# A written-out step list drawn up anew, with 38 constant products at PE's start in place of 28

## The chip, the cores and the metric

The kernel runs on one core of a Trainium2 chip. Its time is the device time of one execution in microseconds (us). The engines are PE (TensorE, matrix products), ACT (ScalarE), DVE (VectorE), POOL (GpSimd) and SP (SyncE, which here only issues transfers). Each engine works through its own instructions strictly in the order in which they were written down, and waits on semaphores for the others.

## The reference

```python
x = A_x                                              # 2048 x 512, bf16
g = sigmoid((x * gate_w).sum(-1, keepdims=True))
# a: state space layer with 512 complex states
Lam_bar = exp(dt * Lam);  Bu = x @ B_bar.T
h[t] = Lam_bar * h[t-1] + Bu[t]                      # t = 0 .. 2047
a = 2.0 * (h @ Cmat.T).real + x * Dskip
# b: linear attention, 32 heads of 16, softmax features
q, k, v = split(x @ wqkv);  pq, pk = q @ w_phi, k @ w_phi    # per head
phi = concat(softmax(p), softmax(-p))                # for q and for k
kv = phi_k.T @ v;  z = phi_k.sum(seq)
b = (phi_q @ kv / (phi_q @ z + 1e-6)) @ wo
return g * a + (1 - g) * b
```

## The kernel before

The sequence is cut into 16 tiles of 128 rows. The rows are dealt out by their index modulo 8 (r = 0..7), so that the recurrence runs over chunks of 8 steps: within a chunk it is made of matrix products, and only the last step of each chunk goes through a scan on DVE.

The work is cut into small generator steps, and each token of the string `ORDER` (line 24) runs the next piece of one step. The order of the tokens is thus the order of every engine's instructions, of SP's transfers too; a scheduler changes nothing on PE, DVE, ACT and SP. A token can carry the PSUM banks (`@6`), and an engine: `:D` puts the evacuation of that piece on DVE in place of ACT, `:A` sends an output through ACT's queue in place of SP's. The loop that does it:

```python
for tok in ORDER.split():
    tok, _, eng = tok.partition(":")
    tok, _, banks = tok.partition("@")
    sel["eng"] = "dve" if eng == "D" else "act"
    sel["q"] = nc.scalar if eng == "A" else nc.sync
    sel["banks"] = [int(b) for b in banks]
    if tok == "F":
        for _ in range(int(eng)):
            MM(out=spin[:, 0:P], lhsT=fillw[:], rhs=fillw[:], start=True, stop=True)
        continue
    next(st[tok])
```

The steps that the prediction names, with their lines in the profile:

- `F:n` (L829): n products of a constant tile with itself, whose results nobody reads.
- `W0..W3` (L277, evacuated at L121 on ACT or L123 on DVE): transposes of the weights of k, in tiles `ptw`, into a part of `Xq`. `f0..f3` (L434): products of these with the block matrix `BD`, in tiles `pf`, evacuated by ACT into `Wk`. `f1` needs `W1` alone, and so on; a `k` needs all four. `w0..w3` are the same for q, from weights that the transfers `Q0..Q3` (L295) bring into `HM`; each `w` needs all four `Q`.
- `V`, `V2` (L313, L320): transposes of the small parameter vectors `vec_n`, `vec_m`, in tiles `pvt`.
- `l8..l15` (L232): transposed loads of x into `xT`, issued by SP. Tiles 0 to 7 are loaded ahead of the list.
- `k0..k15`, `q0..q15` (L478, 4 products of 512 columns): features of keys and queries. `v0..v15` (L492): the values.
- `grj` (L614, L619, L621): input products of the recurrence into `pgq`, from the transposed weights `BT` that the transfers `R0..R7` (L291) bring. `hrj` (L685): the states. `yn` (L734, L739): the output of the state space layer into `py`.
- `xn`, `nn`, `en`, `sn` (L519 to L567): the softmax features of a group of tiles of k; `X`, `N`, `E`, `S` those of q. In `S`, ACT takes a logarithm `lgq` and an exponential `rhoq` (L140), and after `rhoq` DVE scales `EEq` (L567); the result is transposed into `phT`, by SP's transfers (L579) or, for tiles 14 and 15, by PE (`pht`, L574).
- `an` (L594): the sums of the linear attention into `kvacc`.
- `on`: per tile two groups of products `pn` (L753), ACT's logarithm `ld` and exponential `rd` (L140), a cast `nu`, DVE's product `on` (L761), and its transpose `oT` by SP (L775) or PE (`po`, L770). `tn`: the last products `py<-Wo,oT` (L782), the scaling by the gate into `ot` (L786 on ACT, L788 on DVE), and the output transfer (L790).
- `C`, `J`, `c` (L299, L304, L603): the output weights of the state space layer, loaded, rearranged and scaled.

Of the kernel before, what the change touches and what calls it, by code (L numbers as in the profile page):

```python
# [23 lines left out]
ORDER = """
NI l8 l10 F:28 W1@0 W0@1 W0 B W2@2 W2 NR W1:D W3@3 f1@4 f1 W3:D V@5 V U f0@6 U P P P2 U P2 P2 P2 P2 f0 f2@0 P4 P4 P4
V2@1 V2 f2 l9 P3 i3 f3@3 f3 F:4 k1@2 k0@4 P P2 P3 l12 i1 i0 k0 gw i0 i3 U k1 i3 i3:D i3 i0 i1 i1 k2@5 k2 k3@6 k3 v0@03
k4@1 i0:D x0 i1:D l11 x0 i1 n0 F:4 x0 k4 n0 R0 i2 n0 i0 x0 n0 k5@4 i2 i2 x0 i2:D n0 x1 x1 k5 n1 i2 v3@25 v0 x1 k7@6 k7
k6@7 R1 L e0 n1 n1 x1 n1 l13 k6:D v4@14 x1 l14 v1@03 v1 k10@6 n1 x2 v4 n2 n2 n2 x2 e0 s0 x2 v3 v7@70 v7 l15 k8@3 v2@14
v6@25 s0 s0 k9@7 k12@0 x2 Q1 e1 s0 v2 v6 s0 k11@1 s0 e1 M k11 k8 D k10 k9 R3 k12 g40@4 g40 s0 s1 g00@2 g00 n2 a0@51 a0
v5@36 v5 s1 R5 x2 v8@70 R2 v8 C5 s1 s1 s1 s1 g60@4 n2 x3 s1 g60 g30@2 x3 n3 x3 n3 g10@3 C3 g20@6 e2 e2 e2 e2 x3 a1 a1  # L30
n3 Q2 k15@7 g10 g10 k15 x3 n3 g20 k14@0 k14 s2 n3 R4 s2 k13@4 g01@3 Q0 k13 n4 s2 g30 g01 x4 s2 x4 Q3 n4 x4 g50@7 g70@6
g30 g50 n4 x4 e3 e3 g41@0 g50 n4 R7 s2 g21@4 s2 g70 s2 C7 e3 g31@3 e3 s3 g62@2 C4 g70 g70 z0 g11@7 a2 z0 s3 g41 z0 a2
a2 s3 C6 g21 g62 C2 C1 g11 g11 C0 J0 w0@6 w1@0 J2 J2 a2 g22@4 J0 w2@2 x4 s3 J1 g31 w1 w0 w3@7 g22 g31 z0 z0 z0 s3 w2
s3 n4 z0 z0 w3 g61@0 g51@6 g51 g61 g02@4 g51 e4 g02 g71@3 g71 g71 g71 q3@2 s3 g12@7 g12 e4 q2@0 z0 g12 z1 q3 q1@6 q1
q0@4 q2 z1 z0 h50@3 z1 z1 g42@7 q0 z1 z1 v10@26 h50 xA z1 h10@0 e4 e4 z1 g42 nA s4 g32@4 v10 g32 a3 g52@3 g32 h60@7 c2
xA s4 c4 O g52 xA c4 R6 z1 z1 v9@26 s4 h10 g52 nA g72@4 g72 c4 h60 v9 a3 J3 g03@3 v11@26 c2 c2 s4 g72 g72 c0 c0 nA
g63@0 z2 z2 v12@74 a3 nA v11 a3 xA g03 z2 z2 z2 z2 xA nA s4 J3 g63 g23@2 c5 s4 v12 g23 h51@6 g13@3 g13 g13 z2 z2 c0 z2
z2 eA g43@0 g43 eA v14@74 v14 J1 h51 s4 g33@2 g33 h52@3 g33 h12@0 g53@6 eA g53 g53 h12 h11@7 h11 h52 eA sA g73@4 g73
g73 g73 v13@26 v13 q10@0 z3 c6 z3 c5 sA z3 z3 v15@73 z3 a4 a4 a4 v15 z3 q10 q5@4 a4 Y z3 h31@0 q5 sA h30@4 z3 q9@2 h31
q13@6 h31 q9 h33@0 h61@7 Y q13 h30 sA sA c5 h62@3 z3 z3 h30 h61 sA Y Y h22@5 q4@2 h62 q4 h33 q15@6 q11@7 h22 h20@4 h20  # L40
h32@2 h32 sA sA c1 q11 h13@1 h13 h32 q14@3 h40@5 h33 c3 h53@7 h42@4 sA h42 h53 c1 c1 sA h21@2 c3 h21 q6@0 q6 q15 c6
q7@1 h63@4 h63 q8@7 h03@0 c3 q7 c6 h40 sA c7 h41@6 h41 y6@2 c7 h03 h03 h43@4 h43 y2@1 h02@5 c7 sA h23@6 h23 h01@0
h00@4 END q8 G X1 y6 y6 q14 y2 N1 X1 h00 h00 N1 y2 h02 h02 X1 N1 G h01 o0@6 y0@7 o0 o0@3 h01 o2@4 o2 X1 o2@5 o2 o2 N1
y5@6 o0 y3@0 X1 N1 y5 X2 o0 o1@4 E1 o2 y0 o2 o0 E1 E1 E1 X2 y1@5 y1 y3 y3 o1 G N2 X2 N2 X2 o0 N2 X2 o3@3 o3 o3@4 S1 o3
o3 G S1 N2 S1 t2 o3 S1 o3 t2 t2:A q12@3 q12 N2 S1 S1 o1@4 o1 o1 o1 o1 S1 S1 E2 S1 y0 y4@1 y9@3 y8@4 y8 y8 X3 E2 E2 S1
S1 S1 N3 X3 E2 t3 X3 X3 X3 S2 N3 t0 t0 t0:A S2 t3 S2 y1 t1 t1 y5 y9 y9 o4@7 o4 o4@0 o4 y4 o4 o4 o4 o5@5 o5 o5@7 o5 o5
y13@0 S2 S2 o6@5 o6 o6@7 o6 o6 y13 N3 y7@5 y7 N3 y7 y13 o5 S2 S2 N3 E3 o5 o6 o6 S2 S2 E3 E3 o7@7 o7:D y4 t4 t4:D t5
o7@7 S2 S2 E3 S3 t5 S2 S3 S3 o7 o7 o7 t6 y11@1 y11 o7 t6 o8@6 o8 o8@7 o8 o8 S3 S3 o8 y12@2 o9@6 o9 o9@7 o8 y11 y12 y12
y10@6 o9 o9 o9 o11@7 o11 o9 S3 S3 y10 y10 o11@7 t7 o11 o11 t7 t8 S3 S3 o11 o11 S3 t8 S3@7 S3:D S3@5 S3 t9 t9 t1:A
o10@4 y15@7 o10:D o10@5 o10:D t8 o10 o10 o10 y15 o12@4 o12:D o12@3 t4 o14@5 o12 o12 o12 t5 o14 t11 o14@4 o14:D o14 o14  # L50
t11 y14@3 t9:A o13@5 o13 o12@4 o12:D y14 o13@1 o13 o13 o15@4 o15:D o15@5 o15 o15 t12 t3:A t10 o13 o13@1 o15 t6:A t11
o14@4 o13:D t7 t10 t10 y15 t12 t12 o15@5 o15 y14 o14:D t13 t14 t14 t14 t13 t13 t15 t15 t15:A
"""
# [811 lines left out]
```

## Time and profile before

| | us |
|---|---|
| median of 3 runs | 155.99 (155.83 to 156.77) |
| span of the profiled execution | 153.7 |
| PE, ACT, DVE, POOL busy | 145.5, 136.7, 131.0, 12.9 |
| TensorE clock granted, mean over the span | 0.995 |

The page gives the profiled execution its span, from the first to the last instruction of the core, and no time of its own. The runs lie 2.3 us above that span; what is counted there is outside the core's instructions. In a timeline, each row has a start, a length, an engine, a line, an operation, the tiles it writes and reads, and in brackets how long its engine stood idle before it and who ended that. PEld is the loading of PE's stationary operand, and names that end in q (SPq, ACTq) are the engines' transfer issues. Matmuls overlap, so a busy PE in a timeline need not be at its peak.

### The profile page before, as it was taken

What the parts mean: (1) busy time and instruction counts of PE and PEld (TensorE: products, weight loads), DVE (VectorE), ACT (ScalarE), POOL (GpSimd) and SP (SyncE); (2) the same over time, 40 slices, a digit from 0 to 9 for tenths busy, and PEclk for the clock granted to TensorE, in tenths of its full rate; (3) what the DMA queues carried; (4) which work ended last, traced back from release to release, by engine and by line L of the source; (5) the groups of instructions that cost most, each with busy time, mean ns of one, the idle gap of its engine ahead of it and who ended that gap; (6) DMA issues with size and microseconds to landing.
All of it is one profiled execution on the core that took longest, in us unless ns stands there. A gap on an engine that the chain in (4) does not pass through costs nothing.

```text
span 153.7 us, 3412 instructions
## 1 busy us (share of the span) xinstructions
PE 145.5 (95%) x1238; PEld 99.7 (65%) x1254; DVE 131.0 (85%) x302; ACT 136.7 (89%) x322; POOL 12.9 (8%) x43
## 2 busy tenths in 40 slices
PE   7799999999999999999999999999999899999990
...
DVE  3599999999999999999999999999999858445510
ACT  3599999999999999999999999999798897577672
...
GB/s 117 162 220 121 213 171 102 102 86 92 101 102 100 80 146 205 237 133 0 2 4 2 0 0 134 125 18 68 33 82 118 215 80 194 141 118 172 211 123 102
DMA packets 48737, 17.03 MB, mean 111 GB/s; under 512 B 42064, under 2 KB 48720, under 8 KB 48720
## 3 DMA queue, kind: packets, MB, share of 16 engines
...
q8 instruction: 10, 0.16, 0.5%
...
q14 instruction: 7, 0.06, 0.1%
...
## 4 chain that ended last, share of the span: by engine, by line
ACT 48%; PE 31%; DMA 8%; DVE 6%; issue 3%; POOL 2%; ACTq 0%; POOLq 0%
PE py L734 12%; ACT EEk L140 12%; ACT uv L121 9%; PE py L782 6%; ACT vx L121 5%; PE pq L478 5%; ACT Xq L121 5%; ACT phT L603 4%; PE ph L685 3%; ACT va L121 3%; DMA phT<-EEq 3%; DMA oT<-on 3%; PE pn L753 2%; DMA vec_n<-in_A_log_dt_dram 2%; ACT EEq L140 2%
## 5 line engine op out<-in xcount | busy, mean ns | idle before, releaser
L614 PE MATMUL pgq<-xT,BT 128*128 128x256 bf16 x256 | 31.5, 272 | 0.0
L614 PEld LDWEIGHTS <-BT 128*128 128x128 bf16 x256 | 24.7, 98 | 3.5
L140 ACT ACTIVATE EEk<-EEk 128x1024 bf16<-128x1024 bf16 x20 | 21.3, 1099 | 0.0
L478 PEld LDWEIGHTS <-xT 128*128 128x128 bf16 x128 | 12.2, 97 | 11.0 <-issue 0.2
L121 ACT CAST uv<-pgq 128x512 bf16<-128x512 f32 x28 | 16.7, 638 | 0.0
L492 PE MATMUL pv<-Wv,xT 128*128 128x256 bf16 (+1 forms) x128 | 16.5, 273 | 0.1
L478 PE MATMUL pq<-Wq,xT 128*128 128x512 bf16 x60 | 15.2, 379 | 0.2
L782 PE MATMUL py<-Wo,oT 128*128 128x512 bf16 x59 | 14.7, 379 | 0.6 <-DMA oT<-on 0.3
L478 PE MATMUL pk<-Wk,xT 128*128 128x512 bf16 x60 | 14.9, 379 | 0.2
L492 PEld LDWEIGHTS <-xT 128*128 128x128 bf16 x128 | 12.5, 98 | 3.1 <-issue 0.2
L786 ACT ACTIVATE ot<-py,G 128x512 bf16<-128x512 f32 x15 | 9.8, 684 | 2.9 <-PE py L782 2.4
L140 ACT ACTIVATE EEq<-EEq 128x1024 bf16<-128x1024 bf16 x12 | 11.8, 1084 | 0.3 <-DVE EEq L535 0.3
L603 ACT ACTIVATE phT<-X,dgB 128x512 bf16<-128x512 bf16 x16 | 11.1, 751 | 0.0
L140 ACT ACTIVATE ld<-pn 128x16 f32<-128x16 f32 x32 | 6.4, 204 | 5.2 <-PE pn L753 5.0
L121 ACT CAST vx<-pv 128x256 bf16<-128x256 f32 x32 | 10.7, 435 | 0.0
L121 ACT CAST nu<-pn 128x256 bf16<-128x256 f32 x26 | 10.0, 400 | 0.0
L556 DVE TENSOR_TENSOR EEk<-EEk,rck 128x4096 bf16<-128x4096 bf16 (+1 forms) x5 | 9.3, 1860 | 0.1
L121 ACT CAST Xq<-pq 128x512 bf16<-128x512 f32 x16 | 9.0, 604 | 0.4 <-PE pn L753 0.4
L782 PEld LDWEIGHTS <-oT 128*128 128x128 bf16 x64 | 5.7, 98 | 5.7 <-DMA oT<-on 0.5
L753 PEld LDWEIGHTS <-phT 128*128 128x128 bf16 x128 | 6.4, 97 | 4.6 <-DMA phT<-EEq 1.3
L761 DVE TENSOR_TENSOR on<-nu,rd 128x512 bf16<-128x512 bf16 x16 | 6.6, 422 | 2.6 <-ACT rd L140 2.1
L519 DVE TENSOR_TENSOR smk<-smk 128x512 bf16<-128x512 bf16 (+4 forms) x18 | 8.1, 449 | 0.1
...
## 6 DMA issues: line engine op xcount, KB each, us to landing
...
```

Source lines behind the costliest of these rows:

```text
L121: nc.scalar.copy(out=out_ap, in_=in_ap)
L140: ins = nc.scalar.activation(**kw)
L478: MM(out=pt[:], lhsT=xT[:, kt, ti * P:(ti + 1) * P], rhs=W[:, kt, :], start=(kt == 0), stop=(kt == KT - 1))
L492: MM(out=pv[c][:], lhsT=xT[:, kt, ti * P:(ti + 1) * P], rhs=Wvg[:, kt, c * hd:(c + 1) * hd + c], start=(kt == 0), stop=(kt == KT - 1))
L519: VT(out=dst, in0=cur[:, :, :, 0:n, :], in1=cur[:, :, :, n:2 * n, :], op=op)
L556: VT(out=E5, in0=E5, in1=rc.to_broadcast([P, L, 2 * NB, Dh, 4]), op=ALU.mult)
L603: nc.scalar.mul(out=t_, in_=x_, mul=c_)
L614: MM(out=pg[:, h, :], lhsT=BT[:, kt, 2 * j + h, :], rhs=xT[:, kt, r * NC:(r + 1) * NC], start=(h == 0 and kt == 0), stop=(r % 2 == 0 and k ...
L734: MM(out=py[:], lhsT=hs(r, t, slice(a * P, (a + 1) * P)), rhs=C2B[t], start=(t == 0), stop=False)
L753: MM(out=pn[:, 4 * m:4 * m + 4, :].rearrange("p h e -> p (h e)"), lhsT=ph[:, 4 * hf + m, :], rhs=KVm[:, 4 * hf + m, :], start=(m == 0), st ...
L782: MM(out=py[:], lhsT=oT[:, g, :], rhs=Wo[:, g, :], start=False, stop=(g == HG - 1))
L786: nc.scalar.mul(out=ot[:], in_=py[:], mul=G[:, ti:ti + 1])
```

## The change

Only the string `ORDER` differs. It still has 865 tokens, and every step has the same pieces. What differs is their order, the PSUM banks, the engine of 20 pieces, the queue of 4 outputs, and the first count of constant products:

```diff
-NI l8 l10 F:28 W1@0 W0@1 W0 B W2@2 W2 NR W1:D W3@3 f1@4 f1 W3:D V@5 V U f0@6 U P P P2 U P2 P2 P2 P2 f0 f2@0 P4 P4 P4
...
-o14@4 o13:D t7 t10 t10 y15 t12 t12 o15@5 o15 y14 o14:D t13 t14 t14 t14 t13 t13 t15 t15 t15:A
+NI B F:38 W0@5 W0 W1@2 W1:D W2@6 W2:D W3@2 W3:D f1@1 f1 l10 V@0 V U f3@6 P f0@4 f3 P f0 l8 f2@3 f2 NR l9 l12 l11 U P2
...
+o13 t10:D t12 o15@1 t13 t12:D t12 o15:D o14 t14 t10:A t14:D t13 t13:A t3:A t15 t15:D t4 t15:A t14
```

By its tokens, the evacuation of `W2` goes from ACT to DVE. In the last stretch the scaling of `t4` comes to ACT, that of `t8` to `t12`, `t14` and `t15` goes to DVE, and some casts and copies of `o7`, `o10` and `o12` to `o15` change sides. Of the seven outputs in ACT's queue, those of `t9` and `t6` change places with those of `t10` and `t13`.

**ACT at the program's start.** `ptw` are the transposed weights of k (`W`), `pf` the folded ones (`f`). Before:

```order
L132 ACT_TABLE_LOAD
L121 COPY Xq<-ptw 128x4x128 x2
L121 CAST Wk_78<-pf 128x512
L140 ACTIVATE ssm_par<-vec 128x4
L121 CAST Wk_78<-pf 128x512 x3
L140 ACTIVATE ssm_par<-ssm_par 128x4
```

Now:

```order
L132 ACT_TABLE_LOAD
L121 COPY Xq<-ptw 128x4x128
L121 CAST Wk_78<-pf 128x512
L140 ACTIVATE ssm_par<-vec 128x4
L121 CAST Wk_78<-pf 128x512 x3
L140 ACTIVATE ssm_par<-ssm_par 128x4
```

One of ACT's two evacuations of `W` is gone (DVE has three now, not two), and the rest of this stretch stands as it stood. On PE, the 16 products of `W` and the 16 of `f` follow the 38 constant products; `V` stands behind four products of `f` as before, and `V2` behind all sixteen, not behind twelve.

**SP's queue, from the eighth of the x tiles on.** `xT<-in_A_x_dram` are the `l` transfers, `BT<-Bn` the `R`, `HM<-in_B_wqkv_dram` the `Q`. Before:

```order
L287 DMA Bn<-in_A_B_re_dram 64x8x512
L232 DMA_TRANSPOSE xT<-in_A_x_dram 128x4x128 x3
L291 DMA_TRANSPOSE BT<-Bn 128x4x128 x2
L232 DMA_TRANSPOSE xT<-in_A_x_dram 128x4x128 x3
L295 DMA_TRANSPOSE HM<-in_B_wqkv_dram 128x512
L291 DMA_TRANSPOSE BT<-Bn 128x4x128 x3
L299 DMA_TRANSPOSE HM<-in_A_C_im_dram 128x512 x2
L295 DMA_TRANSPOSE HM<-in_B_wqkv_dram 128x512
```

Now:

```order
L287 DMA Bn<-in_A_B_re_dram 64x8x512
L232 DMA_TRANSPOSE xT<-in_A_x_dram 128x4x128 x3
L291 DMA_TRANSPOSE BT<-Bn 128x4x128 x2
L232 DMA_TRANSPOSE xT<-in_A_x_dram 128x4x128
L295 DMA_TRANSPOSE HM<-in_B_wqkv_dram 128x512 x2
L291 DMA_TRANSPOSE BT<-Bn 128x4x128 x2
L232 DMA_TRANSPOSE xT<-in_A_x_dram 128x4x128 x2
L295 DMA_TRANSPOSE HM<-in_B_wqkv_dram 128x512
L299 DMA_TRANSPOSE HM<-in_A_C_re_dram 128x512
L295 DMA_TRANSPOSE HM<-in_B_wqkv_dram 128x512
```

The last two tiles of x (first `l15`, then `l14`) stand behind four other transfers that they stood ahead of, or that stood further back; the fourth `Q` is the tenth transfer from `l13` on, where it was the thirteenth.

**ACT near the end, in the last group of query features.** `lgq` and `rhoq` are the logarithm and exponential of that group, `ld`, `nu`, `rd` those of a tile of `o` (tile numbers differ between the programs). Before:

```order
L140 ACTIVATE lgq_2237<-smq1_2188 128x256
L140 ACTIVATE ld_2247<-pn_2249 128x16
L121 CAST nu_2246<-pn_2249 128x256
L140 ACTIVATE ld_2247<-pn_2256 128x16
L121 CAST nu_2246<-pn_2256 128x256
L140 ACTIVATE rd_2248<-ld_2247,nge_85 128x128
L140 ACTIVATE ld_2286<-pn_2288 128x16
L121 CAST nu_2285<-pn_2288 128x256
L140 ACTIVATE rhoq_2299<-dlq_2297 128x128
```

Now:

```order
L140 ACTIVATE ld_2254<-pn_2256 128x16
L121 CAST nu_2253<-pn_2256 128x256
L140 ACTIVATE lgq_2275<-smq1_2196 128x256
L140 ACTIVATE ld_2254<-pn_2267 128x16
L121 CAST nu_2253<-pn_2267 128x256
L140 ACTIVATE rd_2255<-ld_2254,nge_85 128x128
L140 ACTIVATE rhoq_2295<-dlq_2293 128x128
L140 ACTIVATE ld_2300<-pn_2302 128x16
```

`rhoq` now stands ahead of the following tile's first `ld`, not behind it and its cast.

More of the change, by code (lines that the diff above doesn't have):

```diff
@@ L24 @@
 ORDER = """
-NI l8 l10 F:28 W1@0 W0@1 W0 B W2@2 W2 NR W1:D W3@3 f1@4 f1 W3:D V@5 V U f0@6 U P P P2 U P2 P2 P2 P2 f0 f2@0 P4 P4 P4
[L26 to L49, printed above, removed]
@@ L50 @@
-o10@4 y15@7 o10:D o10@5 o10:D t8 o10 o10 o10 y15 o12@4 o12:D o12@3 t4 o14@5 o12 o12 o12 t5 o14 t11 o14@4 o14:D o14 o14
-t11 y14@3 t9:A o13@5 o13 o12@4 o12:D y14 o13@1 o13 o13 o15@4 o15:D o15@5 o15 o15 t12 t3:A t10 o13 o13@1 o15 t6:A t11
-o14@4 o13:D t7 t10 t10 y15 t12 t12 o15@5 o15 y14 o14:D t13 t14 t14 t14 t13 t13 t15 t15 t15:A
+NI B F:38 W0@5 W0 W1@2 W1:D W2@6 W2:D W3@2 W3:D f1@1 f1 l10 V@0 V U f3@6 P f0@4 f3 P f0 l8 f2@3 f2 NR l9 l12 l11 U P2
+P2 P2 R0 R1 U l13 P2 P2 Q1 Q0 P4 P P3 P4 V2@0 F:4 V2 P4 U i3 i1 R2 i0 gw k0@6 k1@4 P2 k0 R3 l15 i0 k1 i3 i3 i0 k2@2
@@ new lines @@
+l14 i1 k3@5 i3:D i1 v0@10 n0 i3 x0 n0 k3 k4@6 v0 x0 i2 F:4 k5@1 P3 k6@3 Q2 k2 x0 C0 k4 n0 v1@06 i0:D i0 x0 n0 x0 k5 i2
+x1 i1:D i2 i1 i2:D i2 Q3 n0 x1 L C3 n1 k6:D n1 x1 k7@4 k7 n1 v3@71 x1 n1 x1 n1 R4 n2 R5 x2 C4 v4@25 v1 k8@3 e0 v7@40
+e0 n2 v4 C5 x2 v7 k10@6 k8 M s0 s0 v3 v2@25 x2 C7 s0 n2 s0 s0 D C6 v2 k9@0 k9 v6@43 s0 s0 k12@5 e1 e1 k12 k11@7 g40@2
+g40 v6 g00@0 s1 a0@51 s1 k11 n2 s1 R6 a0 g00 x2 s1 k10 v5@42 x2 g60@7 n2 x3 s1 v5 g20@6 n3 s1 s1 g60 v8@20 x3 n3 e2 e2
+g01@3 g10@4 a1 v8 a1 x3 e2 e2 g10 n3 k15@2 x3 C2 n3 k14@7 g20 k13@0 x3 g30@6 g10 k14 g30 k15 s2 s2 g01 n3 g50@2 s2 k13
@@ new lines @@
+n4 g30 w0@7 s2 e3 g50 x4 C1 g50 n4 J0 x4 J1 n4 J2 x4 J3 s2 s2 e3 e3 e3 g21@4 s2 g11@6 g31@3 n4 s3 x4 g70@0 s3 g70 g70
+g70 g41@2 a2 g11 g41 a2 a2 z0 z0 a2 g62@0 s3 w1@2 g21 z0 s3 g22@4 g11 g31 w1 s3 g62 w0 g31 x4 s3 z0 z0 z0 g61@6 w2@2
+w2 g61 g51@0 g51 g51 w3@3 w3 n4 e4 g71@7 g71 z0 z0 g71 g22 q1@6 g71 q0@0 s3 q0 q2@2 z0 q2 q1 g02@3 z1 g02 z1 q3@0 z0
+z1 q3 J2 J0 g12@7 e4 J3 g12 z1 z1 z1 g12 nA xA v10@64 z1 z1 g42@3 nA h50@2 h50 e4 e4 h10@0 h10 v10 s4 z1 z1 xA g32@7
+g32 g42 s4 g52@2 J1 v9@60 c4 g32 g52 h60@3 c2 h60 s4 v9 nA g52 g72@4 h51@6 h51 c4 c5 xA g72 v11@02 g72 h11@3 c4 a3 s4
@@ new lines @@
+a3 a3 v11 h11 xA g72 z2 z2 a3 nA c2 R7 g03@0 v12@74 xA nA g63@2 s4 c0 c0 g03 g63 v12 eA g23@3 g23 g13@0 g13 z2 h61@6
+z2 z2 s4 c2 g43@4 g13 z2 g43 eA g33@7 g33 g33 v14@34 v14 g53@0 c0 z2 z2 eA h61 g53 z2 g53 z2 s4 eA h52@7 h52 g73@6 g73
+h12@3 g73 q10@4 g73 sA q10 h31@4 h62@0 h62 v13@27 c6 z3 sA v13 h12 z3 h32@3 q9@6 sA q13@0 a4 z3 q9 h31 h31 v15@72 a4
+h32 c5 z3 v15 z3 z3 sA h22@6 h32 z3 z3 a4 q5@4 q13 q5 h22 h41@7 a4 Y c3 q4@2 q4 z3 z3 sA q7@0 h20@6 q7 h41 h30@0 sA sA
+c5 c1 h42@4 h42 c1 c3 O h20 Y q6@2 q6 h53@7 q15@3 h53 sA q8@4 h30 h30 h13@5 q15 h13 h21@6 q8 q14@7 c1 h21 sA q11@0
@@ new lines @@
+h40@4 h33@3 q14 h63@2 c6 Y h33 h33 h23@5 c3 y0@7 c7 c7 Y q11 h63 y2@1 c6 h23 sA sA h03@0 h40 c7 h43@6 h02@3 y6@2 y6
+h43 h03 h00@5 sA h01@6 END h03 h02 h02 X1 y6 N1 h00 X1 y0 G N1 X1 N1 h01 h00 h01 o0@0 o0 o0@4 o0 y2 X1 o2@5 o2 o2@3 N1
+o2 o2 o0 y5@6 X1 N1 X2 o2 y5 X2 y5 E1 E1 E1 E1 o1@3 o1 y3@0 y0 N2 o3@4 o3 y3 y3 X2 o2 G y1@5 y1 o3@3 y2 t2 N2 o0 o0 X2
+o3 q12@4 o3 N2 X2 o1@3 o1 o1 S1 G S1 o3 t0 S1 N2 S1 S1 N2 y1 S1 o1 q12 o3 G o1 S1 S1 S1 E2 E2 y9@3 S1 y9 X3 X3 y8@4 N3
+t2 E2 E2 X3 y8 t3 y4@1 t1 t0 y4 t3 t1 o4@7 o4 o4@0 y4 y9 y8 o4 o4 o5@5 N3 X3 o5 o5@7 o5 X3 o5 S2 S2 N3 S1 y13@0 S2 o4
```

5 lines of the change are left out of this document (added).

## The prediction

> **What bounds the kernel now.** I read the page's summary first, then the busy time by stage, then the timelines of the places where the list is changed.
>
> ```profile
> PE 145.5 (95%) x1238; PEld 99.7 (65%) x1254; DVE 131.0 (85%) x302; ACT 136.7 (89%) x322; POOL 12.9 (8%) x43
> PE   7799999999999999999999999999999899999990
> DVE  3599999999999999999999999999999858445510
> ACT  3599999999999999999999999999798897577672
> ```
>
> PE, DVE and ACT are all full from the third slice to about the thirtieth of 40; in the last quarter only PE is. How full, the stages tell (start to end, length, then busy time and instructions of PE, PEld, DVE, ACT, POOL):
>
> ```profile
> 0.00:8.40 8.40, 6.26 (x66) 5.65 (x67) 4.20 (x28) 4.06 (x8) 4.15 (x14) 1.00 0.56 132
> 8.40:20.00 11.60, 11.49 (x74) 6.91 (x74) 11.39 (x42) 11.54 (x26) 8.77 (x29) 1.00 1.00 193
> 20.00:40.00 20.00, 19.87 (x175) 14.94 (x176) 19.83 (x38) 19.93 (x51) 0.00 (x0) 1.00 0.61 109
> 40.00:60.00 20.00, 19.94 (x198) 16.46 (x197) 19.71 (x39) 19.82 (x38) 0.00 (x0) 1.00 0.60 113
> 60.00:85.00 25.00, 24.58 (x255) 20.68 (x256) 24.81 (x55) 24.79 (x60) 0.00 (x0) 1.00 0.34 72
> 85.00:100.00 15.00, 14.90 (x93) 8.59 (x93) 14.71 (x33) 14.97 (x30) 0.00 (x0) 1.00 0.35 68
> 100.00:116.00 16.00, 15.89 (x113) 8.32 (x114) 15.76 (x35) 15.03 (x37) 0.00 (x0) 1.00 0.26 60
> 116.00:121.00 5.00, 4.59 (x43) 2.35 (x40) 4.70 (x9) 3.87 (x14) 0.00 (x0) 1.00 1.18 162
> 121.00:132.00 11.00, 10.89 (x91) 6.04 (x93) 7.67 (x13) 9.84 (x29) 0.00 (x0) 1.00 0.65 144
> 132.00:137.00 5.00, 4.61 (x41) 2.65 (x40) 2.28 (x4) 2.46 (x9) 0.00 (x0) 1.00 0.47 99
> 137.00:148.80 11.80, 11.69 (x113) 6.96 (x113) 5.94 (x14) 8.50 (x28) 0.00 (x0) 1.00 0.69 173
> 148.80:153.70 4.90, 0.82 (x4) 0.20 (x2) 0.00 (x0) 1.84 (x3) 0.00 (x0) 0.85 0.32 107
> ```
>
> Between 8.4 and 100 us, 91.6 us long, PE is busy 90.8, ACT 91.1 and DVE 90.5: idle 0.8, 0.5 and 1.1 us. From 100 to 148.8 PE idles 0.11 + 0.41 + 0.11 + 0.39 + 0.11 = 1.1 us. The list moves work and takes none away, so its room is small: 1.9 us of idle PE, the 8.4 us before PE's first `k`, and the 4.9 us from 148.8 on, in which the last products, their scaling and the last output follow each other. Against that, a delay put in before 100 us finds no slack on any of three engines to hide in, and reaches the end in full.
>
> **The start: 0.5 us later.** The opening of PE, and the evacuations behind it:
>
> ```profile
> 1.12 3.17 PE L829 MATMUL spin<-fillw 128*128 128x128 bf16 x28 [1.12 <-DVE fillw L159]
> 4.32 1.61 PE L277 MATMUL ptw<-ident,C2r 128*128 128x128 bf16 x16
> 6.78 0.16 PE L313 MATMUL pvt<-ident,vec_n 12*128 12x12 bf16 x1 [0.63 <-DMA vec_n<-in_A_log_dt_dram]
> 7.85 0.16 PE L320 MATMUL pvt<-ident,vec_m 8*128 8x8 bf16 x1 [0.35 <-DMA vec_m<-in_gate_w_dram]
> 8.18 0.39 PE L829 MATMUL spin<-fillw 128*128 128x128 bf16 x4
> 5.97 0.42 DVE L123 COPY Xq<-ptw 128x512 bf16<-128x512 bf16 x1 [0.57 <-PE ptw L277]
> 6.35 0.60 ACT L121 CAST Wk<-pf 128x512 bf16<-128x512 f32 x1
> 7.31 1.65 ACT L121 CAST Wk<-pf 128x512 bf16<-128x512 f32 x3
> ```
>
> The 28 constant products take 3.17 us, some 0.107 each from start to start; the four at 8.18 take 0.39 with the length of the last, some 0.056. So the products of the first microseconds run at half the rate. The 16 of `W` take 1.61: by those two steps about ten at 0.107 and the rest at 0.056, which puts the change of rate near 5.4 us. (The stage rows give a granted clock of 1.00 even for 0 to 8.4; here I go by the products' spacing.) Ten more constant products at 0.107 end at 1.12 + 38 x 0.107 = 5.2 us. `W` starts there, 0.9 later than at 4.32, but meets the full rate after two or three products: three at 0.107 and thirteen at 0.056 are 1.05 us, to 6.2. `W3` now takes `W1`'s bank, and must wait for that evacuation: `W1` is through at 5.8, DVE begins some 0.2 later and takes 0.42, to 6.4. So `W3` runs from 6.4 to 6.65, and its evacuation, behind the other two on DVE, to 7.3. `f1` follows at 6.65, then `V` at 6.9 without a wait, since its transfer is there (the row of 6.78 waited for it); then `f3` at 7.3, `f0`, `f2` to 8.0, `V2` without a wait (its transfer came by 7.85), and the four constant products to 8.3. ACT takes up `f1` at 7.1, the small exponential at 7.55, and the other three from 7.7 at 0.53 each: the last ends at 9.3, where it ended at 7.31 + 1.65 = 8.96. The first `k` needs its `f`s in the order 0, 1, 2, 3, so it starts at 8.8, waits some 0.1 for `f2`, and ends at 9.75, against 8.40 + 4 x 0.216 = 9.26 before. **+0.5 us.** The bounds: 0, if the longer opening only fills the waits of 0.63 and 0.35; 1.07, if all ten products come on top. The evacuation of `W2` that ACT gives to DVE is in this walk.
>
> The Trainium skill bears on this in "TensorE: Matmul & The Clock Gate", Part 1: the full clock comes some 3.4 us of sustained work after PE begins, moved by up to 0.5 us by where a free-running window falls, and counts time, not products. By that rule ten more products buy no earlier clock; a change of rate half a microsecond sooner would shorten this term from 0.5 to some 0.35, one later would lengthen it. The trace's 5.4 us agrees.
>
> **SP's queue: 0.4 us later.** The transfers of x that move, and what PE does when it wants them:
>
> ```profile
> 24.53 3.88 SPq L232 DMA_TRANSPOSE xT<-in_A_x_dram  x3
> 29.77 4.56 SPq L291 DMA_TRANSPOSE BT<-Bn  x3
> 36.97 1.26 SPq L295 DMA_TRANSPOSE HM<-in_B_wqkv_dram  x1
> DMA to landing us min/median/max: 2.9/4.0/5.7
> 34.41 1.02 PE L478 MATMUL pk<-Wk,xT 128*128 128x512 bf16 x3
> 35.27 0.38 PE L619 MATMUL pgq<-uv,dg 128*128 128x256 bf16 x2
> ```
>
> SP issues a transposed transfer every 1.31 us (three in 3.88) without a break, so a place in the queue is a time. `l13` at 24.53 keeps its place; `l14` goes from the second to the seventh from there, which is the third of the `BT` row, begun at 34.33 - 1.27 = 33.06. Its landing, by the row on `xT`, is 2.9 to 4.0 us later: 36.0 to 37.1. On PE the three last `k` begin at 34.41 now. Ahead of them stands the same work in both lists but for the two carry products of the row at 35.27, which now come first (0.22). So `k15` starts at 34.41 + 0.5 + 0.22 = 35.1 and `k14` at 36.0, where `l14` may land or may be 1.1 us short. `l15`, one place ahead, is 1.3 us sooner for a `k` that is 0.9 sooner, and costs less. Behind `k14` in PE's order stand all input products, for which uv's evacuations on ACT wait, and behind its evacuation the features of that group of four on DVE; neither has idle time. I take 0.4, from 0 to 1.1, since the loads issued after 20 us meet a quieter queue than the early ones in that median. The fourth `Q` comes at the tenth place, 36.97, and `w0` follows `k14` by about 4 us of PE work, so it costs nothing more unless it lands over 3.3 us later.
>
> **8.4 to 100 us otherwise: 0.** The same work in another order, on engines idle 0.5 to 1.1 us of 91.6. At best all 0.8 of PE's idle time goes; at worst a list with a like number of small misses adds as much again. I keep it at 0, from -0.8 to +0.8.
>
> **The last third: 0.4 us sooner.**
>
> ```profile
> 119.83 0.43 PE L753 MATMUL pn<-KVm,phT 128*128 128x68 bf16 x8 [0.36 <-DMA phT<-EEq]
> 133.20 0.18 ACT L140 ACTIVATE ld<-pn 128x16 f32<-128x16 f32 x1 [1.17 <-PE pn L753]
> 133.89 1.23 DVE L567 TENSOR_TENSOR EEq<-EEq,rhoq 128x2048 bf16<-128x2048 bf16 x1 [1.20 <-ACT rhoq L140]
> 134.72 1.69 PE L782 MATMUL py<-Wo,oT 128*128 128x512 bf16 x7 [0.34 <-DMA oT<-on]
> 148.80 1.84 ACT L786 ACTIVATE ot<-py,G 128x512 bf16<-128x512 f32 x3 [1.10 <-PE py L782]
> L788 DVE TENSOR_SCALAR ot<-py,G 128x512 bf16<-128x512 f32 x1 | 0.7, 742 | 0.0
> ```
>
> Here DVE and ACT have room, and the waits come from the order: ACT stands 1.17 us before an `ld` whose products PE has not done, and `rhoq`, on which the whole last group of features hangs, stands behind it; DVE then waits 1.20 for `rhoq`. In the new list `rhoq` is ahead of that `ld`, so the features and the transposes of the last four tiles come about a microsecond sooner against the rest. PE gains by it only what it now waits. The 0.39 of 132 to 137 is mostly one wait, for the `oT` transfer of the seventh tile, which keeps its place in SP's queue behind four transfers of `phT`. So the gain lies in the later waits and in that of 119.83, and is below the 1.1 us of idle PE: I take 0.4. The bounds are 1.1 gained and 0.6 lost, the latter if the first `phT` copy, which goes from DVE to ACT, holds up the products behind it, and the wait of 119.83 comes again elsewhere.
>
> **The end: 0.06.** The last scaling is DVE's at 0.74 us in place of ACT's (three in 1.84), then an output through ACT's queue as before. Between 0 and 0.3, if DVE's copy of the last `po` delays it.
>
> **The sum.** 0.5 + 0.4 + 0 - 0.4 + 0.06 = +0.56 us: a span of 154.2, against the profiled execution's 153.7. The runs' median is 2.3 us above that span, which I leave as it is: **156.5 us**, 0.3% slower, and inside the 1% (1.6 us) that a measurement of this kernel tells from no change.
>
> **The rivals.**
>
> *The late transfers decide, slower.* The place is `k14`. If `l14` lands 4.0 us after its issue or later, three full engines stand behind it; with the start's ten products in full and the middle's misses the sum is 1.07 + 1.1 + 0.3 - 0.2 = 2.3, so 158.3. It passes 1% when `l14` lands 1.1 us late and the last third gives nothing back. For it: the queue has no break, so any hitch (three `BT` issues took 4.56, where three usually take 3.88) moves all that follow. Against it: a landing of 3 us is seen in this queue too. Chance 0.33.
>
> *The waits go, faster.* If the idle time of PE from 8.4 to 148.8 shrinks to a fifth (-1.5), with a start at 0.2 and no wait at `k14`: and 0.2 off the last output: -1.5 + 0.2 - 0.2 = -1.5, so 154.5. For it: the waits of ACT and DVE at 133 are of the order's making. Against it: it needs nearly every hole closed in a list that leaves 2%. Chance 0.16.
>
> *The change does not do what its words say.* If PE's instruction packets are what these rows of the waits show (what waits, on what, us in total, times, longest), the stops come after so many instructions, whatever these are:
>
> ```profile
> PEld L685 <- issue: 0.5, 2, 0.3
> PEld L619 <- issue: 0.4, 1, 0.4
> ```
>
> A new order then only moves them; start and end cancel, 156.0. Chance 0.1, within 1% as well.
>
> *The forecast,* 0.41. So faster 0.16, same 0.51, slower 0.33. The range of 8 in 10 goes from 154.6 to 158.4; it holds the forecast's own, 155.6 to 157.5, and most of the two cases beside it.
>
> **What would show it.** The first `k` group should end near 9.75 us, with 38 constant products to 5.2 and no wait at `V`. PE should stand at the load of `xT` ahead of the second of the last three `k`, near 36 us, for some tenths. From 40 to 100 us the three engines should be as full as now. DVE's wait for `rhoq` should be gone, its scaling of the last group near 133 us in spite of the later start. PE's last product should end near 150.2, not 149.6. Wrong it is if PE's idle time between 8.4 and 100 us is over 2 us, if the queue delays PE by more than 1.1 us, or if the last third loses time.

## The result, and the profile after

The changed kernel takes 158.26 us (157.52 to 158.59, median of 4 runs); the kernel before took 156.03 us beside it. The ratio is 1.0118, with a 95% interval of 1.0086 to 1.0150: 1.2% slower, or 1.8 us. (The two medians lie 2.2 us apart; from here on I go by the ratios.) The forecast was 156.5, 0.3% slower. The time lies in the range, 0.1 us from its upper end, at the figure of the rival with the late transfers (158.3); the forecast itself had a third of the loss or less.

The profiled execution of the changed kernel spans 156.2 us, 2.6 more than that of before (156.22 against 153.65). In the runs that have both on record, the time is 2.0 us above the span, where I had 2.3 from a median; so the profiled execution of before took some 155.7, just under the fastest of its timed runs. The page of the change and its busy time by stage, at the same places as before:

```profile
PE 147.5 (94%) x1264; PEld 99.6 (64%) x1264; DVE 133.2 (85%) x304; ACT 135.0 (86%) x320; POOL 14.4 (9%) x43
8.40:20.00 11.60, 10.94 (x68) 6.28 (x67) 11.42 (x42) 11.54 (x28) 7.01 (x21) 1.00 1.06 174
20.00:40.00 20.00, 19.57 (x167) 14.06 (x168) 19.33 (x37) 19.37 (x47) 3.24 (x9) 1.00 0.63 115
40.00:60.00 20.00, 19.68 (x196) 16.13 (x195) 18.84 (x37) 19.15 (x37) 0.00 (x0) 1.00 0.67 135
60.00:85.00 25.00, 24.99 (x243) 20.79 (x241) 24.44 (x51) 24.80 (x57) 0.00 (x0) 1.00 0.27 59
85.00:100.00 15.00, 15.00 (x109) 8.82 (x107) 14.76 (x35) 14.94 (x32) 0.00 (x0) 1.00 0.26 51
```

From 20 to 40 us all three engines are now idle, 0.43, 0.67 and 0.63 us, where it was 0.13, 0.17 and 0.07. Stops that all three share point to a delay from outside. After 60 us PE is full again.

The total of PE's busy time (147.5 against 145.5) misleads: the rows on a timeline merge, and 16 products lack a record in the trace of before. A cleaner measure is how late PE is against its own work: the start of a product, less what all products ahead of it in the program take at their closest spacing (0.216 us for 512 columns, 0.109 for 256, 0.056 for 128, 0.031 for 68). Both lists have the same products but for ten constant ones, whose 0.56 us is added. The changed kernel's lateness less that of before, in us, at a few times of the two traces:

```
at          12    22    31    38    42    60    98   118   124   139   144   149
later by  0.06  0.90  0.79  1.37  1.86  1.67  1.72  1.49  0.94  1.34  2.10  2.77
```

So it is lost in three places: 0.9 near 20 us, 1.1 from 31 to 42, and 1.3 from 118 on, with 1.4 behind 139 alone; 0.4 comes back on the way from 42 to 118.

**The start.** PE's rows in the first ten microseconds:

```profile
1.12 3.56 PE L829 MATMUL spin<-fillw 128*128 128x128 bf16 x38 [1.12 <-DVE fillw L159]
4.51 0.93 PE L277 MATMUL ptw<-ident,C2r 128*128 128x128 bf16 x12
6.76 0.16 PE L313 MATMUL pvt<-ident,vec_n 12*128 12x12 bf16 x1 [0.51 <-DMA vec_n<-in_A_log_dt_dram]
7.87 0.16 PE L320 MATMUL pvt<-ident,vec_m 8*128 8x8 bf16 x1 [0.17 <-DVE ssm_par L351]
8.41 2.38 PE L478 MATMUL pk<-Wk,xT 128*128 128x512 bf16 x10
```

The ten more products cost nothing here: all 38 are done at 4.7, since the rate doubled near 3.8 us and not at 5.4, and `V`, `V2` and the first `k` stand where they stood (6.78, 7.85, 8.40). I had counted the waits for the vectors as gone; that of `V` is there.

**PE's stops from 20 to 42 us.** These are the rows of PE and of its loads with a wait for a transfer:

```profile
20.17 1.04 PE L478 MATMUL pk<-Wk,xT 128*128 128x512 bf16 x4 [0.82 <-DMA xT<-in_A_x_dram]
33.81 1.49 PE L614 MATMUL pgq<-xT,BT 128*128 128x256 bf16 x12 [0.25 <-DMA BT<-Bn]
36.85 1.41 PEld L478 LDWEIGHTS <-xT 128*128 128x128 bf16 x8 [0.46 <-DMA xT<-in_A_x_dram]
41.43 0.23 PE L434 MATMUL pf<-BD,HM 128*128 128x128 bf16 x1 [0.32 <-DMA HM<-in_B_wqkv_dram]
```

The second is for `R3`, the third for `l14`, the fourth for the last `Q`. In lateness they are 0.42, 0.13 and 0.49 us (the bracket counts only from the modelled end of the product before). Before, PE had none of them; 32 input products ran in one row without a wait:

```profile
30.41 3.65 PE L614 MATMUL pgq<-xT,BT 128*128 128x256 bf16 x32
```

The queue behind the stops in the change:

```profile
25.45 1.26 SPq L232 DMA_TRANSPOSE xT<-in_A_x_dram  x1
26.76 2.56 SPq L295 DMA_TRANSPOSE HM<-in_B_wqkv_dram  x2
29.37 3.17 SPq L291 DMA_TRANSPOSE BT<-Bn  x2
32.58 2.57 SPq L232 DMA_TRANSPOSE xT<-in_A_x_dram  x2
35.20 1.26 SPq L295 DMA_TRANSPOSE HM<-in_B_wqkv_dram  x1
36.50 1.26 SPq L299 DMA_TRANSPOSE HM<-in_A_C_re_dram  x1
37.81 1.26 SPq L295 DMA_TRANSPOSE HM<-in_B_wqkv_dram  x1
```

The first is `l13`, at 25.45 and not at 24.53. `R3` is the second of the row at 29.37, issued near 31.3; it lands just before PE goes on at 33.81. `l14` is the second of the row at 32.58, issued near 33.9; it lands at 36.8, as PE goes on.

**The last third.**

```profile
125.11 1.04 PE L782 MATMUL py<-Wo,oT 128*128 128x512 bf16 x4 [0.34 <-DMA oT<-on]
135.88 0.29 PE L753 MATMUL pn<-KVm,phT 128*128 128x68 bf16 x4 [0.31 <-ACT nu L121]
141.93 0.43 PE L753 MATMUL pn<-KVm,phT 128*128 128x68 bf16 x8 [0.22 <-DMA phT<-EEq]
142.55 1.04 PE L782 MATMUL py<-Wo,oT 128*128 128x512 bf16 x4 [0.19 <-DMA oT<-on]
146.54 0.29 PE L753 MATMUL pn<-KVm,phT 128*128 128x68 bf16 x4 [0.28 <-DVE nu L123]
128.91 1.22 DVE L519 TENSOR_TENSOR smq<-EEq 128x2048 bf16<-128x2048 bf16 x1 [3.06 <-ACT EEq L140]
133.58 0.42 ACT L140 ACTIVATE lgq<-smq 128x256 f32<-128x256 f32 x1 [0.82 <-DVE smq L519]
135.01 1.22 DVE L567 TENSOR_TENSOR EEq<-EEq,rhoq 128x2048 bf16<-128x2048 bf16 x1
149.64 2.75 PE L782 MATMUL py<-Wo,oT 128*128 128x512 bf16 x12
151.57 1.61 DVE L788 TENSOR_SCALAR ot<-py,G 128x512 bf16<-128x512 f32 x2 [0.87 <-PE py L782]
```

DVE's wait for `rhoq` is gone: the scaling at 135.01 stands behind its neighbour without a wait. But the wait only changed its name. DVE waits 3.06 us for the exponentials of that group on ACT, and ACT 0.82 for DVE's sums. The scaling comes at 135.01 where it came at 133.89. With PE 1.3 us later altogether, that leaves it 0.2 us ahead, not a microsecond. Behind it PE has four stops near 142 and 146.5 of 0.2 to 0.45 us each in lateness. From PE's last product (152.39) to the end it is 3.8 us; before it was 4.0 (149.62 to 153.65), so the last scaling on DVE gains 0.2.

### The profile page after: what moved, and what is told of

It reads as the page before. It is cut to its first block, busy times and chain, and to the rows that moved or that the text cites. A ratio compares the mean times of both kernels' runs of the same rounds, so it can differ in the third digit from the quotient of the medians.

```text
span 156.2 us, 3452 instructions
## 1 busy us (share of the span) xinstructions
PE 147.5 (94%) x1264; PEld 99.6 (64%) x1264; DVE 133.2 (85%) x304; ACT 135.0 (86%) x320; POOL 14.4 (9%) x43
## 3 DMA queue, kind: packets, MB, share of 16 engines
HBM read 2.64 MB, written 2.10 MB: 30 GB/s over the span
## 4 chain that ended last, share of the span: by engine, by line
PE 64%; SPq 19%; DMA 11%; ACT 2%; issue 1%; DVE 1%; DVEq 0%
PE py L734 14%; PE pgq L614 13%; SPq L232 11%; PE pq L478 9%; PE py L782 8%; DMA oT<-on 4%; PE ph L685 4%; DMA Bn<-in_A_B_re_dram 4%; PE pv L492 4%; SPq L291 4%; SPq L295 2%; DMA HM<-in_B_wqkv_dram 2%; PE kvacc L594 2%; PE pgq L619 2%; PE pn L753 2%; PE pgq L621 2%
## 5 line engine op out<-in xcount | busy, mean ns | idle before, releaser
L782 PE MATMUL py<-Wo,oT 128*128 128x512 bf16 x64 | 15.9, 379 | 0.5 <-DMA oT<-on 0.5
L478 PE MATMUL pk<-Wk,xT 128*128 128x512 bf16 x64 | 15.5, 379 | 0.9 <-DMA xT<-in_A_x_dram 0.8
L121 ACT CAST nu<-pn 128x256 bf16<-128x256 f32 x30 | 11.1, 393 | 0.0
L121 ACT CAST Xq<-pk 128x512 bf16<-128x512 f32 x15 | 8.7, 599 | 0.3 <-PE pk L478 0.2
L788 DVE TENSOR_SCALAR ot<-py,G 128x512 bf16<-128x512 f32 x7 | 5.2, 750 | 4.0 <-PE py L782 3.9
```

The lines of the kernel that those rows point to most:

```text
L121: nc.scalar.copy(out=out_ap, in_=in_ap)
L478: MM(out=pt[:], lhsT=xT[:, kt, ti * P:(ti + 1) * P], rhs=W[:, kt, :], start=(kt == 0), stop=(kt == KT - 1))
L782: MM(out=py[:], lhsT=oT[:, g, :], rhs=Wo[:, g, :], start=False, stop=(g == HG - 1))
```

## The experiments

All but the change itself, whose row is that of the section above, were timed in five rounds beside the kernel before on the same chip; its median there was 156.7 to 156.8, where it was 156.03 beside the change. So rows are compared by the ratio. The ratio is to that kernel, with its 95% interval; microseconds are the ratio's difference times 156. The edits stand as parts of the step list.

| | us | ratio to before |
|---|---|---|
| the change | 158.26 | 1.0118 (1.0086 to 1.0150) |
| change, `l8` ahead of `l10` | 157.97 | 1.0079 (1.0047 to 1.0112) |
| change, 28 constant products | 158.39 | 1.0093 (1.0060 to 1.0125) |
| before, 38 constant products | 156.78 | 0.9986 (0.9965 to 1.0007) |
| change up to `END`, then before | 159.61 | 1.0178 (1.0139 to 1.0216) |
| before up to `END`, then change | 161.43 | 1.0280 (1.0236 to 1.0325) |
| change, queue reordered | 156.82 | 1.0009 (0.9982 to 1.0037) |
| change, only `R2` and `R3` early | 157.98 | 1.0052 (1.0021 to 1.0082) |
| queue reordered but for `Q3` | 157.66 | 1.0055 (1.0030 to 1.0080) |
| before, `l14` late | 157.42 | 1.0025 (0.9995 to 1.0055) |
| change, end of before | 157.99 | 1.0080 (1.0052 to 1.0108) |
| change, queue reordered and end of before | 156.39 | 0.9979 (0.9956 to 1.0003) |
| the same, early loads reordered too | 156.38 | 0.9973 (0.9950 to 0.9995) |

**The stop near 20 us.** It waits for the load of tile 8, which the change put behind that of tile 10.

```diff
-NI ... l10 ... l8 ... NR
+NI ... l8 ... l10 ... NR
```

> The changed list with one exchange in SP's queue: the load of x tile 8 again ahead of that of tile 10; everything else stays. In the profile of the change PE stops 0.99 us at 19.08, before the k of tile 8, whose load was issued at 15.18 and landed at 20.13. Theory (the place in the queue is the price): tile 8 is issued near 13.85 and lands near 19.6, the stop shrinks to some 0.4 us; the k of tile 9 then stands 0.6 us nearer to its own landing (23.25) and may give 0.15 back. So 0.4 to 0.6 us less than the change: 157.7 to 157.9, about 1.009 of before. Rival (ACT or DVE is the bound there and PE's stop is only shown on PE, or the stop moves to the next load): no change, 158.3. That the hitch of 0.67 us in SP's issue at 11.07 is what makes tile 8 late, and not its place, would show as a stop of the same 0.99 us only where the tile still lands at 20.1.

It measured 1.0079: 0.6 us less by the ratio, but the two intervals overlap widely. In its profile the stop has shrunk as expected (0.44 us in lateness for 0.99), but its opening ran 0.35 us later and the next load adds a stop of 0.16; the queue then stops PE longer than in the profile of the change (columns as above):

```profile
19.98 1.04 PE L478 MATMUL pk<-Wk,xT 128*128 128x512 bf16 x4 [0.27 <-DMA xT<-in_A_x_dram]
23.66 0.61 PE L478 MATMUL pk<-Wk,xT 128*128 128x512 bf16 x2
34.22 1.48 PE L614 MATMUL pgq<-xT,BT 128*128 128x256 bf16 x12 [0.66 <-DMA BT<-Bn]
38.08 1.90 PE L478 MATMUL pk<-Wk,xT 128*128 128x512 bf16 x8 [0.78 <-DMA xT<-in_A_x_dram]
```

At 31 us PE is as late against its own work as in the profile of the change, to 0.02 us. So what the place of `l8` is worth is not settled by this run.

**The opening.** Undone in the changed list, and done alone in the list of before:

```diff
-F:38
+F:28
```

> The changed list with 28 constant products at PE's start in place of 38, nothing else. In the profile of the change the first k group starts at 8.41, where it started at 8.40 before. Theory (the ten products fill waits that are there anyway, for the weights' transfer to 4.28, for the first vector transfer to 6.65, for the second to 7.72): no change, 158.3, the first k at 8.4 again, the waits at 4.3, 6.7 and 7.8 back. Rival (they are paid for and only hidden by something else of the new opening): 0.5 us less, 157.7, the first k near 7.9. A second rival (the full rate comes later with fewer products): some 0.2 us more, with the products at 0.107 us apart past 5.4 us.

```diff
-F:28
+F:38
```

> The list of before with 38 constant products at PE's start, nothing else: the term of 0.5 us (0 to 1.07) of the prediction by itself, apart from the new order of W and f. In before, PE waits 0.30 for the weights at 4.32, 0.63 for the first vectors and 0.35 for the second, and 12 of the products of f stand ahead of the last wait. Theory (the ten products, 1.07 us at the slow rate, fill the 0.30 and the 0.63, and what is left over goes into the wait of 0.35): as before, 1.000, first k near 8.4 to 8.6. My prediction's kind of step: 0.3 to 0.5 more, 1.002 to 1.003. Rival (the ten come on top): 1.0 more, 1.0065.

Undone in the changed list it measured 1.0093, 0.4 us less than the change with intervals that overlap widely; done in the list of before it measured 0.9986, which puts the ten products alone at -0.2 us, between -0.5 and +0.1. So no price for them is seen. The first `k` began at 9.26 and at 8.67 in these profiles, where I expected 8.4 and 8.4 to 8.6, and the end does not show it. What hides it is the next load of x: where the opening runs late, the stop near 20 us shrinks by about as much. In the profile of the run with queue and end reordered the first `k` begins at 9.38 and there is no stop near 20; in that of the run with the queue alone, at 8.32, and the stop is 1.15 us in lateness. (In two others the first `k` begins at 8.54 and 9.12 and the stop is 1.21 and 0.81: when that load lands scatters too.)

That also clears up the 0.9 us near 20 us. The list of before with 38 products is, in its profile, 1.2 us later there than the profile of before, yet no slower than before in the times. The profiled execution of before was an early one in this stretch; so the loss at 20 us is, as far as these runs tell, mostly the comparison of single executions.

**The two halves exchanged.** At `END`, near 100 us, both lists have done the same pieces but for three.

> The changed list up to the token END (near 100 us; the same pieces are done there in both lists but for three), and from there the list of before; one piece of h01 moved ahead by three tokens so that its bank is free. Of PE's loss against its own work, 118 to 149 us cost 3.3 us with the change and 2.3 before, in stops ahead of oT, phT and pn. Theory (the new last third itself loses 1.0 us, its end gains some 0.2): 0.8 us less than the change, 157.4 to 157.6, about 1.0085 of before. Rival (the stops of the last third are handed on by what comes late from before 100 us and come again in any order): 158.3. Second rival (the new tail is as good as the old, and the loss is noise of one profile): 158.2.

> The list of before up to the token END, and from there the changed list (the three pieces that differ are put in at the joint). The counterpart of the run with the old tail. Theory (the new last third loses 1.0 and its end gains 0.2): 0.8 us more than before, 156.8, about 1.005. Rival (the loss lies in the first 45 us alone): as before, 156.0. My prediction's own step for this part (0.4 gained): 155.6.

Both came out slower than either parent (158.8 to 160.4 us with the old tail, 159.8 to 161.8 with the new), and tell nothing of the tails by their times. The joint itself stalls: PE stops at each for an evacuation on ACT, which the order of the other half had not put off so long. The first row is from the run with the new tail, the second from that with the old:

```profile
100.17 1.02 PE L734 MATMUL py<-C2r,H 128*128 128x512 bf16 x4 [2.50 <-ACT Xq L121]
```

```profile
104.14 0.67 PE L753 MATMUL pn<-KVm,phT 128*128 128x68 bf16 x16 [1.14 <-ACT Wk L121]
```

So this joint was a poor choice; the next cut lies where the lists agree but for one output.

**The queue.** Only SP's order changes.

```diff
-l13 Q1 Q0 R2 R3 l15 l14 Q2 C0 Q3 C3
+l13 R2 R3 l15 l14 Q1 Q0 Q2 Q3 C0 C3
```

> The changed list; only SP's queue from the load of x tile 13 on is reordered: the two transfers Q1 and Q0 go behind R2, R3, l15 and l14 (which thus come 2.6 us sooner), and Q3 ahead of C0 (1.3 us sooner). All other engines keep their order. Of the profile of the change, PE stops 0.42 us at 33.3 for R3, 0.13 at 36.5 for l14 and 0.49 at 40.9 for the last Q; in the three runs with the change's first half since, these stops were 0.9 to 1.8 us together. Theory (the places in the queue are the price there): the three stops go, no new one comes, since every transfer but Q1 and Q0 is earlier, and Q0 goes where l14 was (issued near 34, landed near 37, wanted near 40): 0.9 to 1.3 us less, 157.1 of 158.3, about 1.004 of before. Rival (PE's stops there only shift ACT's and DVE's work, which are as full, or the DMA engines' load sets the landing whatever the order): no change, 1.010.

1.0009: the order of eight transfers gives back 1.7 us, and the two intervals are apart. In the profile PE has no stop for a transfer between 21 and 42 us. The third row is `w0`, on time:

```profile
33.16 1.91 PE L614 MATMUL pgq<-xT,BT 128*128 128x256 bf16 x16
35.64 2.75 PE L478 MATMUL pk<-Wk,xT 128*128 128x512 bf16 x12
40.41 0.39 PE L434 MATMUL pf<-BD,HM 128*128 128x128 bf16 x4
31.00:42.00 11.00, 11.00 (x105) 8.77 (x103) 10.97 (x20) 11.00 (x24) 0.00 (x0) 1.00 0.52 99
```

From 31 to 42 us PE, DVE and ACT are busy 11.00, 10.97 and 11.00 of 11 us. In the change it is this (same columns):

```profile
31.00:42.00 11.00, 10.43 (x95) 7.65 (x93) 10.80 (x19) 10.35 (x21) 0.00 (x0) 1.00 0.51 101
```

Which of the places costs what, two further runs divide. The first is an edit of the changed list, the second of the run just shown:

```diff
-l13 Q1 Q0 R2 R3 l15 l14 Q2 C0 Q3
+l13 R2 R3 Q1 Q0 l15 l14 Q2 C0 Q3
```

> The changed list; in SP's queue only R2 and R3 go ahead of Q1 and Q0 (2.6 us sooner), while l15, l14, Q2, C0 and Q3 keep their places. The reordering of the whole piece of the queue gave back 1.7 us (1.0009 where the change has 1.0118). Theory (the transfers lie on one queue, and PE meets each later one with the time won at the one before: the last late one decides): the stop at R3 (0.42 in the profile of the change) goes and comes again at l14 and Q3, which land as before: 0 to 0.3 us less, 1.010 to 1.012. Rival (the stops are independent, and R3, which my prediction gave no price, is the largest): 0.4 to 0.8 us less, 1.007 to 1.009.

```diff
-l13 R2 R3 l15 l14 Q1 Q0 Q2 Q3 C0
+l13 R2 R3 l15 l14 Q1 Q0 Q2 C0 Q3
```

> The run on the queue with one exchange undone: R2, R3, l15, l14 stand early, but C0 stays ahead of Q3 as in the changed list. Q3 is issued near 37 us and lands near 41, where with the exchange it lands near 40; w0, which needs all four Q, stands on PE near 39.9. Theory (the last late transfer decides): a stop of about 1 us at w0, and most of the gain of the queue is gone: 0.7 to 1.1 us more than that run, 1.005 to 1.008. Rival (independent stops, Q3 worth the 0.49 of the profile of the change): 1.004. Third (the Q of w0 have slack through what ACT and DVE still have to do): 1.001.

`R2` and `R3` alone give 1.0 us back by the ratio, with intervals that just fail to meet (1.0086 to 1.0150 and 1.0021 to 1.0082); the rival, at 0.4 to 0.8, was nearer than the theory, at 0 to 0.3. The stop at `R3` is gone, and the one at `l14` has grown to 1.2 us in lateness in this profile, as the theory has it. With `l15` and `l14` early as well, but the last `Q` still behind `C0`, nothing more is won (1.0055), and the stop is at `w0` (0.34 us in lateness in its profiled execution, which was the fastest of its runs):

```profile
36.04 1.04 PE L478 MATMUL pk<-Wk,xT 128*128 128x512 bf16 x4
38.14 1.90 PE L478 MATMUL pk<-Wk,xT 128*128 128x512 bf16 x8 [1.06 <-DMA xT<-in_A_x_dram]
```

```profile
40.00 0.33 PE L434 MATMUL pf<-BD,HM 128*128 128x128 bf16 x3
40.51 0.23 PE L434 MATMUL pf<-BD,HM 128*128 128x128 bf16 x1 [0.17 <-DMA HM<-in_B_wqkv_dram]
```

Moving that one transfer, `Q3`, past `C0` is worth the last 0.7 us (1.0055 against 1.0009, with intervals that just overlap). So both readings hold in part: the stops hand on from one to the next, and `R3` and the last `Q` each have to come sooner for the whole 1.7. For `l14` that is argued from its stop of 1.2 us above; no run has it alone late.

The term of the prediction by itself, in the list of before:

```diff
-l13 l14 l15 Q1 R3 R5 R2
+l13 l15 Q1 R3 R2 R5 l14
```

> The list of before with one transfer moved: the load of x tile 14 from the second to the seventh place from that of tile 13, behind l15, Q1, R3, R2 and R5, which come one place sooner. This is the term of 0.4 us (0 to 1.1) of the prediction by itself. l14 is then issued near 33.05 and lands at 36.0 to 37.1; the k that wants it stands at 35.3 in this list. Theory (a late landing stops PE, and the end is later by that stop): 0.7 to 1.7 us more than before, taken 1.0: 1.006. Rival (what follows on ACT and DVE has slack for it, or the earlier R3, R2 and R5 give it back): as before, 1.000. My prediction's estimate of 0.4 would be 1.0026.

1.0025: 0.4 us, the prediction's figure, but anything from -0.1 to 0.9 is inside the interval. Its profile shows the stop, larger than that in this execution, whose queue began 1.2 us later than in the profile of before:

```profile
37.50 1.90 PE L478 MATMUL pk<-Wk,xT 128*128 128x512 bf16 x8 [0.78 <-DMA xT<-in_A_x_dram]
```

**The end.** The changed list up to the twelfth piece of the last `S`, then the list of before:

```diff
-S3 o10@5 o10:D t9 o10@4 y15@7 o10 t9:D ...
+S3 t0:A S3@5 S3 t9 t9 t1:A o10@4 y15@7 o10:D ...
```

> The changed list up to the twelfth piece of the last group's features (S3, near 137 us, where both lists have done the same pieces but one output), and from there the list of before. In the change PE stops at 141.9 (phT, 0.39), 142.5 (oT, 0.36), and at 146.5 and 146.9 (a cast of nu and an on on DVE, 0.44 and 0.21); the loss against its own work from 137 us to the end is 1.8 us, and 0.7 with the list of before. Theory (the order of the last 15 us is the price): 0.9 us less than the change (1.1 of stops, less the 0.2 that the new end gains by its last scaling on DVE): 157.4, about 1.006 of before. Rival (phT and oT come late from before, whatever the order behind): the stops at phT and oT stay and only the 0.65 of the others goes, less 0.2: 157.8. Second rival (a joint that stalls, as the one near 100 us did by 1.6 to 2.7 us): over 158.3, with one stop of more than a microsecond near 137 to 140.

> Both edits in one: the changed list with the reordered queue of the run on the queue, and the end of before from S3 on. Theory (the two losses are independent stops of PE): the sum, 1.0 + 0.9 = 1.9 us less than the change, 156.4, about 1.0 of before. Rival (what is gained before 45 us is lost again in waits of the last third, since the transfers and ACT there keep their time): no more than the better of the two alone, 157.1 to 157.4.

The old end gives 0.6 us back on the change and 0.5 on top of the queue, less than the 0.9 expected. In both pairs the intervals overlap; that the two agree is what speaks for a loss of this size. Of PE's stops there those for `phT`, for `nu` on DVE and for `on` are gone, and one or two of 0.16 to 0.55 for an `oT` are left; that at the second `pn` of its tile (0.31 for `nu` on ACT) lies ahead of the cut and stays. The two edits add up: 0.9979, 1.7 us of the queue and 0.5 of the end. What is left of the new list then is 0.3 us faster than before, as fast as it within the interval.

**All together.**

```diff
-NI l10 l8 NR l9 l12 l11 R0 R1 l13 ...
+l8 NI l10 NR l9 l12 l11 l13 R0 R1 ...
```

> The changed list with all that the runs so far point to: the reordered queue from R2 on, the end of before from S3 on, and ahead of them the load of x tile 8 as the first of the list, that of tile 10 between the two loads of Bn, and that of tile 13 ahead of R0, in the 1.8 us in which SP stands at R0 until Bn has landed; R0 and R1 keep their time, and all from R2 on comes another 1.3 us sooner. The run with queue and end measured 0.998 of before. Theory (PE's stop at the k of tile 8, 0 to 1.15 us in the profiles, goes, and that at the k of tile 9 stays at up to 0.4): 0.3 to 0.6 us less than that run, 155.8 to 156.1, about 0.995 of before. Rival (what the early loads win is lost at the next landing, tile 9 or R1): 0.998 again.

0.9973, no better than the run without it, which was the rival's figure. The stop at the `k` of tile 8 is gone, and the next load takes its place:

```profile
19.94 1.02 PE L478 MATMUL pk<-Wk,xT 128*128 128x512 bf16 x4
24.05 1.04 PE L478 MATMUL pk<-Wk,xT 128*128 128x512 bf16 x4 [0.30 <-DMA xT<-in_A_x_dram]
```

Nor did the rest of the queue come 1.3 us sooner: `R2` is issued at 26.20, where it was 26.66 with queue and end alone, since SP waits at `R0` for the second half of `Bn`, and that landed at 23.57 and not at 22.71. This kernel and the one without the early loads are the fastest of the study and not told apart; against before its interval (0.9950 to 0.9995) just leaves out no change, with 0.4 us.

## Why the prediction was right or wrong

The way was right, and the size was short: 0.56 us forecast, 1.8 measured. In place of the terms 0.5, 0.4, 0, -0.4 and 0.06 the runs put nothing for the start, 1.7 for the queue, 0.5 for the last 15 us with the end, and -0.3 for all the rest.

**What bounds the kernel: right from 30 us on.** PE, DVE and ACT are full together, and what stops PE between 30 and 42 us reaches the end: 1.7 us came back when those transfers came sooner.

**The start, 0.5: wrong, it costs nothing** (-0.2, between -0.5 and +0.1, for the ten products; the new order of `W` and `f` was not tried alone). I walked the opening as if each step were passed on, up to the first `k`. The walk's times are those of one moment of the rate change. And the step that failed lies behind it: "a delay put in before 100 us finds no slack on any of three engines". Near 20 us PE waits for a load of x (up to 1.2 us in these profiles), and an opening of 0.9 us more or less ends in that wait.

**SP's queue, 0.4: the mechanism was right, the size wrong, 1.7.** The term for `l14` alone agrees (0.4 in the list of before, between -0.1 and 0.9). What was mis-sized is the rest of the queue. First, `R3`: I asked only which transfers go back in the queue and not which consumers stand close. `R2` and `R3` went behind two `Q`, and the prediction lets their consumers come late: "Behind `k14` in PE's order stand all input products". In both lists many of them stand ahead of it (the 32 at 30.41 before, the 12 at 33.81 now), and among these PE stops for `R3`. That was the largest share, in the order in which the edits were added here. Second, the fourth `Q` was to cost nothing "unless it lands over 3.3 us later" than 36.97: it was issued at 37.81 and landed 3.6 us after that, `w0` came near 40.8 and waited, and one place is worth 0.7. Third, both rest on the time 24.53 for `l13`, from one execution. It was 25.45 in the next, and between 24.73 and 25.95 in those of the experiments whose queue up to `l13` is that of either list. This scatter has one source, which I did not look for. SP stands at `R0` until the second half of `Bn` has landed (a wait of 0.5 to 2.4 us in the 14 profiles). It lands between 21.9 and 23.6 us, and in 13 of the 14 the transfer behind `R1` is issued 2.63 or 2.64 us after that landing; in the other, one issue stalled. So the places from `l13` on are times counted from this landing. The list of before had about one place to spare in this stretch (its run with 38 products shows no stop there with the queue 1.2 us late); the new list had none.

**8.4 to 100 us otherwise, 0: within its bounds.** From 42 to 118 us PE gains 0.4 in the profile, and with queue and end put right the list is 0.3 us faster than before.

**The last third, -0.4: wrong in sign, by the runs +0.5 to +0.6 from 137 us on** (each with an interval that reaches no change). The step that failed is "`rhoq` is ahead of that `ld`, so the features and the transposes of the last four tiles come about a microsecond sooner". `rhoq` went ahead of the `ld`, but it hangs on `lgq`, on DVE's sums and on ACT's exponentials, and these came no sooner; I followed the wait one instruction back and not to its source. Then I put the four new stops near 142 and 146.5 at nothing.

**The end, 0.06: 0.2 gained** in the profile, since one scaling of 0.75 on DVE replaces the last of three in a row on ACT.

**The rivals.** The late transfers decided, as that rival said, to its figure of 158.3, but at three places rather than at `k14`, and with a loss in the last third that it did not have. Its sum has 1.07 for the start, which costs nothing; that it meets the measured time is luck, and so, with it, that the upper end of the range holds that time. What I had named as what would make the forecast wrong came: "if the queue delays PE by more than 1.1 us" (1.7 by the runs, 1.1 in the profile) and "if the last third loses time". Of the other signs, the stop of some tenths at the load for `k14` (0.13) and the end of the wait for `rhoq` came; the first `k` group ended at 9.3 and not at 9.75, with a wait at `V`, and PE's last product at 152.4 and not at 150.2.
